# Weight units placed 128c+p, small products partly on GpSimd, and a new order for a fused attention and channel-mix kernel

## The chip, the core and the metric

The kernel runs on one core of a Trainium2 chip. The core has five engines with programs of their own: TensorE (PE in the profile), VectorE (DVE), ScalarE (ACT), GpSimd (POOL) and SyncE (SP), which here only issues transfers. The metric is the device time of one execution in microseconds (us), as the median of several runs.

## The reference

Two layers in float32. The first is attention with a polynomial feature map and no softmax, over 4 batches, 4 heads, 1088 positions and 32 columns a head; the second mixes channels, over 1088 positions of 128 columns.

```python
def phi(x):                                   # 32 columns -> 8 x 8 = 64 features
    a = einsum('rd,bhsd->bhsr', S1, x); b = einsum('rd,bhsd->bhsr', S2, x)
    return einsum('bhsi,bhsj->bhsij', a, b).reshape(..., 64)
kv = einsum('bhsf,bhsd->bhfd', phi(k), v);  z = phi(k).sum(axis=2)
x = einsum('bhsf,bhfd->bhsd', phi(q), kv) / (einsum('bhsf,bhf->bhs', phi(q), z) + 1e-6)
x = x, heads side by side                     # (4, 1088, 128)
xk = mu_k * x + (1 - mu_k) * x_prev;  xr = mu_r * x + (1 - mu_r) * x_prev    # x_prev: one position earlier
out = sigmoid(xr @ w_r) * (maximum(xk @ w_k, 0) ** 2 @ w_v)                  # 128 -> 1024 -> 128
```

## The kernel before

All work is cut into small tasks, each a function in the kernel. The text `ORDER` lists their calls; the kernel goes through it from left to right, and this sets the order of instructions on every engine, since each engine runs its own instructions in that order and waits on semaphores for what others make. An entry such as `f1.0.2@67` calls `f1(0, 2)` with PSUM banks 6 and 7; a last letter V, A or G in `relu.0.1.A` chooses DVE, ACT or POOL. A bank can be written again only when its last reader is done.

A batch b goes through these tasks.

- Keys. `turn.k` turns k in blocks on DVE (batches 0 and 2); `pt` and `ptev` do so on PE, with an eviction from PSUM, for batches 1 and 3. `kproj` multiplies by the two sketch matrices, `abev` evicts, `kp` forms the 64 features on DVE. `kvmm` sums features times v on PE; `kvev`, `kdmm` and `kvbm` evict, turn and evict the result. `zmm`, `zev`, `wmm` and `wsq` make from the same projections the matrix by which the denominator is computed.
- Queries. `turn.q` turns q on DVE, `abwt` and `abw` project it on PE, `abwev` evicts. `pw` multiplies two of the three projections elementwise, `den` sums and inverts, `an` multiplies by the inverse, `qp` forms the 64 features. They come in two parts (18 and 16 positions of 34 a row) for batch 0 and in one part (`0.34`) for the others. `qtt` and `qt` turn the features on PE, `qttev` and `qtev` evict.
- Attention's output. `xmm` multiplies by kv; `xev`, `xtev` and `xs` bring x into SBUF, with the shifted position. `xk` and `xkt` form the mixed input in bf16 on DVE, `xb` a bf16 copy for the gate.
- Channel mix. The positions of a batch make groups g = 2b and 2b + 1 of 512, and group 8 holds the 256 left over. For each group, `f1.g.c` (c = 0 to 3) makes two blocks of 128 hidden units from `xk` and the scaled weights `wk`; `relu` evicts them to bf16, `sq` squares two of them at once, `f2.g.c` multiplies by `wv`. `rr` and `sig` make the gate on PE and ACT; `fin` multiplies the two on DVE and issues the stores, four a group.

`wset` prepares the weights: `wset.1` scales w_k by 1 - mu_k and casts it to `wk`, `wset.2` does both halves of w_r, `wset.3` casts w_v to `wv`. [...] Which hidden unit lies at which place is free, as long as `wk` and `wv` agree. Before, block c held units 8p + c: `wk_f` is read with a step of NC = 8 columns, and partition p of `wv_f` gets eight rows of w_v that lie side by side in memory.

All loads are issued by SP, in the order k0, q0, v0, the first keys of the turned batches (`krow0`), k1, w_k, q1, v1, w_r, w_v, then k, q and v of batches 2 and 3. Stores of the first seven groups that finish go out on SP; those of the eighth alternate between SP and ACT; the store of group 8, the last, is on SP.

Of the kernel before, what the change touches and what calls it, by code (L numbers as in the profile page):

```python
# [24 lines left out]


ORDER = """
zz.8@7 turn.k.0.0 spe.1@0 turn.k.0.1 spe.0@1 sk wset.4 zz.3@3 kproj.0.0@2 kproj.0.1@1 abev.0.0.A turn.q.0.2 abev.0.1.A
zz.2@4 zmm.0@3 zev.0.V wset.0 zz.1@4 wmm.0 wsq.0 kp.0.1 zz.1@4 abwt.0@2 abw.0.0 kp.0.0 abw.0.1@3 abwev.0.0.A
pt.k.1.1@2 pw.0.0.18 pt.k.1.0@1 ptev.k.1.1.A den.0.0.18 kvmm.0.0@0 abwev.0.1.A ptev.k.1.0.A pw.0.18.34 kvmm.0.1  # L30
an.0.0.18 den.0.18.34 pt.k.1.2@1 kproj.1.0@2 qp.0.0 ptev.k.1.2.A wset.1.A kproj.1.1@1 an.0.18.34 kvev.0.A abev.1.0.A
qp.0.1 kdmm.0 qtt.0@3 abev.1.1.A qt.0.0@45 kvbm.0.A qttev.0.A wset.2.A kp.1.0 qt.0.1@67 qtev.0.0.A zmm.1@3 qtev.0.1.A
kp.1.1 xmm.0.0@45 kvmm.1.0@0 xtev.0.A xev.0.0.A xs.0.G zev.1.V xmm.0.1@67 xb.0.0.A xk.0.0 wmm.1 xev.0.1.A turn.q.1.2
f1.0.0@12 xb.0.2.G f1.0.1@45 xb.0.1.G relu.0.0.A kvmm.1.1 wsq.1 wset.3.G xk.0.1 abwt.1@3 relu.0.1.A abw.1.1@1
turn.k.2.2 f1.0.2@67 abwev.1.1.A abw.1.0 sq.0.0.A kvev.1.V pt.k.3.0@1 abwev.1.0.V pt.k.3.1@2 kdmm.1 ptev.k.3.0.V
f1.1.2@34 ptev.k.3.1.A kvbm.1.V rr.1@5 relu.0.2.A pw.1.0.34 pt.k.3.2@0 den.1.0.34 f1.1.3@12 ptev.k.3.2.A kproj.2.0@6
sig.1 an.1.0.34 kproj.3.1@0 relu.1.2.A qp.1.1 kproj.3.0@5 abev.2.0.A f2.0.0@7 abev.3.0.A qp.1.0 abev.3.1.A f2.0.1
relu.1.3.A f1.0.3@56 qt.1.1@34 turn.q.3.2 relu.0.3.A zmm.3@2 kproj.2.1@1 qtev.1.1.A sq.0.2.V qtt.1@0 f1.1.0@56 zev.3.A
abev.2.1.A qt.1.0@34 qttev.1.A xkt.0 kp.3.1 relu.1.0.A wmm.3 f1.1.1@01 qtev.1.0.A wsq.3 zmm.2@5 turn.q.2.2 abw.3.1@2
zev.2.A relu.1.1.A xmm.1.0@34 kp.3.0 abwt.3@6 xtev.1.A abw.3.0 xev.1.0.A xs.1.A abwev.3.1.A f2.0.2 xk.1.0 xb.1.0.G  # L40
abwev.3.0.A wmm.2 rr.0@2 sq.1.2.A pw.3.0.34 f1.2.0@34 wsq.2 den.3.0.34 f1.2.1@01 kvmm.3.0@5 an.3.0.34 sig.0 abwt.2@6
sq.1.0.V abw.2.0 relu.2.0.A abw.2.1@2 qp.3.0 abwev.2.0.A kvmm.3.1 abwev.2.1.A f2.0.3 kvev.3.A relu.2.1.A pw.2.0.34
kdmm.3 rr.2@6 fin.0 f1.2.2@23 kvbm.3.A kp.2.1 sig.2 qtt.3@4 xmm.1.1@01 relu.2.2.A qt.3.0@56 qp.3.1 xev.1.1.A f2.1.0@2
qttev.3.A qtev.3.0.A f2.1.1 xb.1.1.G xk.1.1 f1.2.3@34 sq.2.0.V f1.3.2@01 relu.2.3.A f2.1.2 qt.3.1@56 kp.2.0 relu.3.2.A
f2.1.3 qtev.3.1.A f1.3.3@34 fin.1 xmm.3.0@01 den.2.0.34 relu.3.3.A xmm.3.1@56 sq.2.2.V kvmm.2.0@2 xtev.3.A xev.3.0.A
kvmm.2.1 xs.3.A xev.3.1.A xk.3.0 xb.3.0.G f1.3.0@34 kvev.2.A rr.3@7 xk.3.1 xb.3.1.G relu.3.0.A kdmm.2 f1.3.1@01
an.2.0.34 f2.2.0@5 sig.3 sq.3.2.V f2.2.1 relu.3.1.A f1.6.0@34 qp.2.1 f2.2.2 relu.6.0.A f2.2.3 f1.6.1@01 fin.2 kvbm.2.A
qt.2.1@67 relu.6.1.A sq.3.0.V f1.7.1@23 qtev.2.1.A f1.7.0@01 qp.2.0 f2.3.0@5 relu.7.0.A f2.3.1 f2.3.2 sq.6.0.V qtt.2@4
relu.7.1.A f1.6.2@01 f2.3.3 qttev.2.V qt.2.0@67 xb.1.2.A sq.7.0.V relu.6.2.A f1.6.3@23 f2.6.0@4 qtev.2.0.V relu.6.3.A
f1.7.2@01 f2.6.1 xkt.1 relu.7.2.A sq.6.2.V xmm.2.0@67 xmm.2.1@23 xtev.2.A xev.2.0.A fin.3 xs.2.G f1.7.3@01 xev.2.1.A  # L50
xb.2.0.G f2.6.2 xk.2.0 relu.7.3.A f2.7.0@5 xb.2.1.G xk.2.1 f1.4.0@67 xb.2.2.A rr.6@0 relu.4.0.A sq.7.2.V f1.4.1@23
rr.7@1 sig.6 f1.4.2@67 relu.4.1.V sig.7 f2.7.1 relu.4.2.A f1.4.3@01 sq.4.0.V f2.6.3 f1.5.2@23 relu.4.3.A f1.5.0@67
fin.6 f2.7.2 relu.5.0.A f1.5.1@01 sq.4.2.V f2.7.3 relu.5.1.A f2.4.0@4 fin.7 f2.4.1 xkt.2 relu.5.2.A f2.4.2 xkt.3
sq.5.0.V f1.5.3@01 f1.8.0@56 relu.5.3.A f1.8.1@23 rr.4@7 relu.8.0.V f2.4.3 xb.3.2.A sq.5.2.V f1.8.2@01 relu.8.1.A
f2.5.0@5 sig.4 f2.5.1 f1.8.3@23 sq.8.0.V relu.8.2.A f2.5.2 fin.4 rr.8@7 relu.8.3.A rr.5@6 f2.5.3 sq.8.2.V sig.5
f2.8.0@4 f2.8.1 sig.8 fin.5 f2.8.2 f2.8.3 fin.8
# [8 lines left out]
def kernel(  # L65
# [147 lines left out]
    def scale(eng, o, i, f):  # L213
        if eng == "A":
            nc.scalar.activation(o, i, COPY, scale=f)  # L215
        else:
            nc.gpsimd.tensor_scalar(o, i, f, 0.0, op0=MUL, op1=ADD)

    def wset(i, eng="G"):
        if i == 4:  # L220
            nc.vector.tensor_mul(ZL[:], _ap(ps["s", 1][:, :D], [[0, 4], [1, D]]), _ap(mz[:], [[1, 4], [0, D]]))
            nc.vector.tensor_copy(mu[:], ps["s", 1][:, 64:66])
            nc.gpsimd.tensor_scalar(omu[:], mu[:], -1.0, 1.0, op0=MUL, op1=ADD)
# [1 line left out]
            nc.gpsimd.tensor_add(nzm[:], omu[:], tmp[:])
        elif i == 0:
            nc.vector.reciprocal(rat[:], nzm[:])
            nc.vector.tensor_mul(rat[:], rat[:], mu[:])
        elif i == 1:
            scale(eng, wk[:], _ap(wk_f[:], [[1, NC], [DFF // 2 + 4, 2], [NC, 64]]), nzm[:, :1])  # L230
        elif i == 2:
            scale(eng, wr[:, 0], wr_f[:], mu[:, 1:])
            scale(eng, wr[:, 1], wr_f[:], omu[:, 1:])
        else:
            copy(eng, wv[:].rearrange("p (y c) d -> p y (c d)", y=2), wv_f[:, :, :DFF // 2])

    def copy(eng, o, i):
        if eng == "A":
            nc.scalar.copy(o, i)  # L239
        else:  # L240
            (nc.gpsimd if eng == "G" else nc.vector).tensor_copy(o, i)  # L241
# [218 lines left out]
    def size(g):  # L460
        return 512 if g < 8 else 256

    def f1(g, cp, banks):
        i, j = banks
        n = size(g)
        h = ps["h", g, cp] = PS[:, i:j + 1:j - i, :n]
        if g < 8:
            x = sb["xk", g // 2, g % 2][:]
        else:
            x = XT[:].rearrange("p u b a -> p (u b a)")  # L470
        for c in range(2):
            nc.tensor.matmul(h[:, c, :], wk[:, 2 * cp + c].rearrange("p y f -> p (y f)"), x, skip_group_check=True)  # L472

    def relu(g, cp, eng):
        if cp % 2 == 0:
# [42 lines left out]
        nc.scalar.activation(r[:, :size(g)], ps["r", g][:, :size(g)], SIGMOID)  # L518

    fins = []  # L520

    def fin(g):
# [5 lines left out]
        nc.vector.tensor_mul(x[:, :n], ps["o", g][:, :n], x[:, :n])  # L528
        if g == 8:
            nc.sync.dma_start(out.rearrange("b (a u) f -> (b a) u f", u=U)[:, U - 2:, :], o[:, :2, :])  # L530
        for c in range(4 if g < 8 else 0):
            dst = out[g // 2].rearrange("(a u) f -> a u f", u=U)[:, 16 * (g % 2) + c:16 * (g % 2) + c + 13:4, :]
            queues[c].dma_start(dst, o[32 * c:32 * c + 32])
# [12 lines left out]

# [28 lines left out]
```

## Time and profile before

| | |
|---|---|
| median of 3 runs | 84.17 us (84.11 to 86.27) |
| profiled execution, its own time | 84.56 us |
| its span, from the first to the last instruction | 82.6 us |
| PE, DVE, ACT, POOL busy, share of the span | 92%, 87%, 78%, 11% |
| instructions | 3382 |
| bytes moved by DMA | 10.43 MB |
| granted clock of TensorE | 1.0 of full speed |

A line of a timeline or of the chain gives the start and the length in us, the engine, the tile and the line of the kernel; "x16" means that so many instructions are taken together. A line of the groups gives the busy time of all instructions of a kind and the mean time of one in ns. All lines are from one profiled execution. L239 and L241 are the lines of the helper `copy`, which many tasks share (ACT, and DVE or POOL); L215 is that of `scale`. f1 is L472, f2 L501, relu on ACT L480, sq L491 and L489, fin L528.

### The profile page before, as it was taken

How to read it: one execution, taken by the hardware profiler on the slowest of the kernel's cores; microseconds unless marked ns; L12 is line 12 of the kernel's file. 1: busy time of each engine (PE TensorE's matmuls, PEld its weight loads, DVE VectorE, ACT ScalarE, POOL GpSimd, SP SyncE). 2: the span in 40 equal slices, each digit the busy share in tenths (PEclk: the TensorE clock that was granted, in tenths of full speed). 3: DMA queues.
4: the chain of work that ended last, by engine and by line, in shares of the span. 5: the costliest groups of instructions: out<-in, count | busy, mean ns of one | idle time of the engine just before them, and what ended most of it. 6: DMA issues, size and time to landing. Idle time of an engine off the chain costs nothing.

```text
span 82.6 us, 3382 instructions
## 1 busy us (share of the span) xinstructions
...
## 2 busy tenths in 40 slices
...
GB/s 29 293 271 290 320 378 365 378 385 366 363 367 90 3 8 0 8 4 12 0 8 39 91 4 32 101 2 20 107 8 0 34 94 8 42 136 76 55 194 69
DMA packets 11441, 10.43 MB, mean 126 GB/s; under 512 B 1954, under 2 KB 9380, under 8 KB 11428
## 3 DMA queue, kind: packets, MB, share of 16 engines
...
q8 instruction: 11, 0.18, 0.9%
...
HBM read 8.00 MB, written 2.23 MB: 124 GB/s over the span
## 4 chain that ended last, share of the span: by engine, by line
PE 73%; ACT 8%; DMA 7%; DVE 4%; issue 1%; SPq 1%; DVEq 0%
PE ps L472 18%; PE ps L501 17%; PE ps L362 8%; DMA q<-in_q_dram 7%; PE ps L425 7%; PE ps L331 5%; PE ps L514 5%; PE ps L437 4%; PE ps L285 3%; ACT wk L215 3%; PE ps L267 3%; ACT qpT L239 2%; DVE qT L246 2%; SPq L124 1%; PE ps L349 1%
## 5 line engine op out<-in xcount | busy, mean ns | idle before, releaser
L480 ACT ACTIVATE k<-ps 128x1024 bf16<-128x1024 f32 (+1 forms) x34 | 32.8, 999 | 2.2 <-PE ps L472 1.7
L501 PEld LDWEIGHTS <-k 128*128 128x128 bf16 x272 | 16.6, 98 | 3.3 <-DVE k L491 0.2
L501 PE MATMUL ps<-wv,k 128*128 128x128 bf16 x272 | 18.6, 219 | 0.0
L491 DVE TENSOR_TENSOR k<-k 128x2048 bf16<-128x2048 bf16 (+1 forms) x16 | 18.3, 1149 | 0.3
L472 PE MATMUL ps<-xk,wk 128*128 128x512 bf16 x64 | 18.2, 379 | 0.1
L300 DVE TENSOR_TENSOR kp<-ab 128x1024 f32<-128x1024 f32 (+1 forms) x8 | 10.6, 1347 | 0.4 <-ACT ab L239 0.4
L398 DVE TENSOR_TENSOR qp<-an,abw 128x1152 f32<-128x1152 f32 (+1 forms) x8 | 10.1, 1279 | 0.1
L425 PE MATMUL ps<-ident,qp 128*128 128x128 f32 x64 | 8.3, 274 | 0.0
L239 ACT COPY qpT<-ps 128x1024 f32<-128x1024 f32 (+1 forms) x10 | 8.1, 831 | 0.0
L472 PEld LDWEIGHTS <-wk 128*128 128x128 bf16 x72 | 6.3, 101 | 2.3 <-issue 0.6
L425 PEld LDWEIGHTS ps<-ident,qp 128*128 128x128 f32 x64 | 7.0, 140 | 1.2 <-ACT q L518 0.4
L362 PE MATMUL ps<-SQ,qT 128*32 128x96 f32 (+1 forms) x160 | 7.4, 253 | 0.0
L241 POOL CAST XB<-X 128x512 bf16<-128x512 f32 (+1 forms) x7 | 4.4, 651 | 26.9 <-ACT X L239 26.9
L178 PE MATMUL ps<-zero 128*128 128x512 bf16 x15 | 5.8, 516 | 1.2 <-DVE warm L141 1.2
L362 PEld LDWEIGHTS ps<-SQ,qT 128*32 128x32 f32 (+1 forms) x160 | 6.5, 126 | 0.3
L445 DVE SCALAR_TENSOR_TENSOR xk<-ps,rat,X 128x512 bf16<-128x512 f32 x8 | 5.8, 743 | 1.0 <-ACT X L239 1.0
L246 DVE STREAM_TRANSPOSE qT<-q 128x1088 f32<-128x1088 f32 x4 | 5.2, 1304 | 1.2 <-DMA q<-in_q_dram 1.2
L239 ACT COPY abw<-ps 128x384 f32<-128x384 f32 (+1 forms) x7 | 3.3, 515 | 3.4 <-PE ps L362 3.4
L285 PEld LDWEIGHTS ps<-SK,kT 128*32 128x32 f32 (+1 forms) x234 | 5.3, 116 | 0.8 <-POOL SQ L211 0.4
L239 ACT COPY ab<-ps 128x320 f32<-128x320 f32 (+1 forms) x8 | 3.1, 444 | 3.5 <-PE ps L285 3.4
L285 PE MATMUL ps<-SK,kT 128*32 128x64 f32 (+1 forms) x234 | 5.8, 224 | 0.0
L528 DVE TENSOR_TENSOR q<-ps,q 128x512 f32<-128x512 f32 x8 | 5.5, 688 | 0.2
...
## 6 DMA issues: line engine op xcount, KB each, us to landing
...
kr<-in_k_dram SPq DMA_DIRECT2D x4, 256.0 KB, 7.5
...
```

What stands on the lines that cost most here:

```text
L178: nc.tensor.matmul(PS[:, banks[0], :], zero[:, :P], zero[:], skip_group_check=True)
L239: nc.scalar.copy(o, i)
L246: nc.vector.transpose(qT[b % 2][:].rearrange("p (w u) a -> p w (u a)", w=2), qin[b][:, :, :n])
L285: nc.tensor.matmul(_ap(o[c], *dst), kT[b % 2][:, m, c], SK[:] if b in TURNPE and m else SK[:].rearrange("p x h r -> p x (h r)"), skip_grou ...
L300: e.tensor_mul(o[:, :4 * (KG[j][1] - KG[j][0])], _ap(a_, list(a_.ap[1:]) + [[0, R]]), _ap(b_, [list(b_.ap[1]), [0, R], list(b_.ap[2])]))
L362: nc.tensor.matmul(_ap(o[c], [[6 * R, 4], [1, 3 * R]], c0), x[:, c], SQ[b][:].rearrange("p h r -> p (h r)"), skip_group_check=True, tile_p ...
L398: nc.vector.tensor_mul(o[:, :s1 - s0], _ap(a_, list(a_.ap[1:]) + [[0, R]]), _ap(b_, [list(b_.ap[1]), [0, R], list(b_.ap[2])]))
L425: nc.tensor.transpose(o[:, h // 2, c:c + P], sb["qp", b, hf][:, s:s + 2].rearrange("p s i j -> p (s i j)"), ident[:])
L472: nc.tensor.matmul(h[:, c, :], wk[:, 2 * cp + c].rearrange("p y f -> p (y f)"), x, skip_group_check=True)
L480: nc.scalar.activation(o, h, RELU)
L491: nc.vector.tensor_mul(o, k1, k1)
L501: nc.tensor.matmul(o[:, i * P:i * P + P], k2[:, 2 * (cp % 2) + c, i * P:i * P + P], wv[:, 2 * cp + c, :], start=(cp == 0 and c == 0 and i ...
```

## The change

Hidden unit 128c + p now lies in block c at place p. `wset.1` therefore reads neighbouring columns of `wk_f`, and `wv_f` is loaded with partition p taking row p of each block of 128 rows, in pieces of 512 bytes where it had pieces of 2 KB. Seven of the `pw` and `an` products go to GpSimd. In the stores of the eighth group to finish, the first stays on SP and the other three go to ACT, where they are issued after everything else in its program. `ORDER` is new as a whole; it lists the same tasks with one `zz` matmul fewer.

```diff
-    wv_f = const.tile([P, 2, DFF // 2 + 4], F32)
-    wk = const.tile([P, NC, 2, 64], BF16)
+    wv_f = const.tile([P, NC, P], F32)
+    wk = const.tile([P, NC, P], BF16)
...
-    nc.sync.dma_start(wv_f[:, :, :DFF // 2], moe_w_v.rearrange("(p y c) d -> p y (c d)", y=2, c=NC // 2))
+    nc.sync.dma_start(wv_f[:], moe_w_v.rearrange("(c p) d -> p c d", p=P))
...
-            scale(eng, wk[:], _ap(wk_f[:], [[1, NC], [DFF // 2 + 4, 2], [NC, 64]]), nzm[:, :1])
+            scale(eng, wk[:].rearrange("p (y c) f -> p y (c f)", y=2), wk_f[:, :, :DFF // 2], nzm[:, :1])
...
-            copy(eng, wv[:].rearrange("p (y c) d -> p y (c d)", y=2), wv_f[:, :, :DFF // 2])
+            copy(eng, wv[:], wv_f[:])
...
-            nc.tensor.matmul(h[:, c, :], wk[:, 2 * cp + c].rearrange("p y f -> p (y f)"), x, skip_group_check=True)
+            nc.tensor.matmul(h[:, c, :], wk[:, 2 * cp + c], x, skip_group_check=True)
...
-    fins = []
+    fins, late = [], []
...
-        queues = (nc.sync, nc.scalar) * 2 if len(fins) > 7 else (nc.sync,) * 4
+        queues = (nc.sync,) + (nc.scalar if len(fins) == 8 else nc.sync,) * 3
...
-            queues[c].dma_start(dst, o[32 * c:32 * c + 32])
+            if queues[c] is nc.scalar:
+                late.append((dst, o[32 * c:32 * c + 32]))
+            else:
+                queues[c].dma_start(dst, o[32 * c:32 * c + 32])
...
+    for dst, src in late:
+        nc.scalar.dma_start(dst, src)
```

The two orders from the first projections to where the third f1 pair stands (before, then after):

```
zz.2@4 zmm.0@3 zev.0.V wset.0 zz.1@4 wmm.0 wsq.0 kp.0.1 zz.1@4 abwt.0@2 abw.0.0 kp.0.0 abw.0.1@3 abwev.0.0.A
pt.k.1.1@2 pw.0.0.18 pt.k.1.0@1 ptev.k.1.1.A den.0.0.18 kvmm.0.0@0 abwev.0.1.A ptev.k.1.0.A pw.0.18.34 kvmm.0.1
an.0.0.18 den.0.18.34 pt.k.1.2@1 kproj.1.0@2 qp.0.0 ptev.k.1.2.A wset.1.A kproj.1.1@1 an.0.18.34 kvev.0.A abev.1.0.A
qp.0.1 kdmm.0 qtt.0@3 abev.1.1.A qt.0.0@45 kvbm.0.A qttev.0.A wset.2.A kp.1.0 qt.0.1@67 qtev.0.0.A zmm.1@3 qtev.0.1.A
kp.1.1 xmm.0.0@45 kvmm.1.0@0 xtev.0.A xev.0.0.A xs.0.G zev.1.V xmm.0.1@67 xb.0.0.A xk.0.0 wmm.1 xev.0.1.A turn.q.1.2
f1.0.0@12 xb.0.2.G f1.0.1@45 xb.0.1.G relu.0.0.A kvmm.1.1 wsq.1 wset.3.G xk.0.1 abwt.1@3 relu.0.1.A abw.1.1@1
turn.k.2.2 f1.0.2@67 ...

zz.2@3 zmm.0@0 zev.0.V zz.1@3 wmm.0 wset.0 wsq.0 zz.1@3 abwt.0@1 abw.0.0 abwev.0.0.A kp.0.1 abw.0.1@0 kp.0.0
pt.k.1.0@1 ptev.k.1.0.A pw.0.0.18.G pt.k.1.1@2 ptev.k.1.1.A kvmm.0.0@3 kvmm.0.1 wset.1.A kvev.0.A kproj.1.0@2 kdmm.0
kvbm.0.A abwev.0.1.V pw.0.18.34.G abev.1.0.A den.0.0.18 an.0.0.18.G den.0.18.34 pt.k.1.2@1 ptev.k.1.2.A qp.0.0
qt.0.0@45 qtev.0.0.A an.0.18.34.V qp.0.1 kp.1.0 kproj.1.1@3 abev.1.1.A kp.1.1 qtt.0@2 qttev.0.A wset.2.A qt.0.1@01
qtev.0.1.A xmm.0.0@23 xtev.0.V xev.0.0.A xs.0.G zmm.1@4 zev.1.A kvmm.1.0@5 kvmm.1.1 xk.0.0 turn.q.1.2 kvev.1.A
xb.0.0.A xmm.0.1@01 xev.0.1.A wmm.1 xb.0.1.G f1.0.0@23 f1.0.1@67 relu.0.0.A relu.0.1.A kdmm.1 wsq.1 abwt.1@4 abw.1.0
abwev.1.0.A abw.1.1@2 f1.0.2@67 rr.0@4 kvbm.1.A abwev.1.1.A pt.k.3.2@5 turn.k.2.2 relu.0.2.A wset.3.G pt.k.3.0@2
sq.0.0.V pt.k.3.1@3 ptev.k.3.2.A xk.0.1 pw.1.0.34.G ptev.k.3.0.A ptev.k.3.1.A f1.0.3@01 ...
```

Over the whole order these tasks change their engine:

| from, to | tasks |
|---|---|
| DVE to GpSimd | pw.0.0.18, pw.0.18.34, an.0.0.18, pw.1.0.34, pw.3.0.34, an.3.0.34, an.2.0.34 |
| ACT to DVE | abwev.0.1, xtev.0, xtev.1, xtev.2, xtev.3, sq.0.0, kvbm.2, xev.2.0, xev.2.1, relu.4.2 |
| DVE to ACT | zev.1, kvev.1, abwev.1.0, ptev.k.3.0, kvbm.1, qttev.2, qtev.2.0, relu.4.1 |
| ACT to GpSimd | xs.1, xs.3 |

The end of the two orders (before, then after):

```
f2.5.0@5 sig.4 f2.5.1 f1.8.3@23 sq.8.0.V relu.8.2.A f2.5.2 fin.4 rr.8@7 relu.8.3.A rr.5@6 f2.5.3 sq.8.2.V sig.5
f2.8.0@4 f2.8.1 sig.8 fin.5 f2.8.2 f2.8.3 fin.8

f2.4.3 relu.8.0.V f1.8.2@67 sq.5.2.V f2.5.0@3 rr.5@4 sig.4 fin.4 relu.8.1.A sq.8.0.V f1.8.3@01 f2.5.1 f2.5.2 f2.5.3
relu.8.2.A relu.8.3.A sq.8.2.V rr.8@0 sig.5 f2.8.0@1 fin.5 f2.8.1 sig.8 f2.8.2 f2.8.3 fin.8
```

49 lines of the change are left out of this document (20 added, 29 removed).

## The prediction

> **What bounds the kernel now.** I read the page first, then the stretches (busy microseconds of PE, PE's weight loads, DVE, ACT and POOL, clock, DMA share, GB/s), then the chain that ended last, in order of time.
>
> ```profile
> span 82.6 us, 3382 instructions
> 14.67:21.89 7.22, 6.32 (x124) 4.91 (x124) 5.74 (x8) 7.13 (x15) 0.21 (x1) 1.00 1.07 373
> 21.89:77.04 55.15, 55.15 (x1103) 42.89 (x1103) 54.32 (x72) 52.30 (x82) 5.85 (x10) 1.00 0.20 54
> 77.04:82.60 5.56, 1.32 (x24) 1.15 (x21) 1.64 (x3) 0.87 (x2) 0.00 (x0) 1.00 0.45 118
> ```
>
> From 21.89 us to 77.04 us PE is busy for the whole 55.15 us at full clock, DVE for 54.32 and ACT for 52.30. There PE's own work sets the pace and two engines stand close behind. So time can be had in three places: the entry before 21.89, the work that PE still has to do after it, and the tail after 77.04. POOL works 5.85 of 55.15 us.
>
> ```profile
> 14.67 2.16 ACT wk L215
> ...
> 16.98 0.60 ACT ab L239 x2
> ...
> 17.92 0.59 ACT wr L215 x2
> 18.51 1.81 ACT qpT L239 x2
> 20.32 0.68 ACT X L239 x2
> ...
> 21.09 0.76 DVE xk L445
> ...
> 21.89 1.02 PE ps L472 x4
> 22.91 0.58 PE ps L331 x32
> 23.50 0.12 PE ps L349 x16
> ...
> 77.06 0.61 ACT q L518
> 77.69 0.69 DVE q L528
> ...
> 78.46 0.42 DVE kr L528
> ```
>
> The chain runs through ACT from 14.67 to 21.00: the weight mix wset.1 (2.16 us), then every eviction that batch 0 needs, in ACT's program order, until xk.0.0 can form the first input of f1. At 21.89 the chain goes over to PE (f1.0.0) and stays there.
>
> **The change, part by part.** I follow each engine's program in the new order: an instruction starts when its engine is free and its inputs are there, and lasts as long as its row says.
>
> ```profile
> 9.47 2.62 DVE L300 TENSOR_TENSOR kp<-ab 128x1024 f32<-128x1024 f32 x2
> 11.13 0.52 ACT L239 COPY abw<-ps 128x432 f32<-128x432 f32 x1 [3.09 <-PE ps L362]
> 12.57 1.21 PE L331 MATMUL ps<-kp,v 128*32 128x64 f32 x72
> 14.10 2.12 PE L285 MATMUL ps<-SK,kT 128*128 128x64 f32 x18
> 17.31 1.91 PE L425 MATMUL ps<-ident,qp 128*128 128x128 f32 x16
> 21.76 1.30 DVE L246 STREAM_TRANSPOSE qT<-q 128x1088 f32<-128x1088 f32 x1
> 23.71 2.15 DVE L249 STREAM_TRANSPOSE kT<-k 128x576 f32<-128x576 f32 x2
> ```
>
> *Weight mix.* A row of the groups by shape (busy, mean ns of one, idle before):
>
> ```profile
> L239 ACT CAST XB<-X 128x544 bf16<-128x544 f32 x1 | 0.6, 645 | 0.1
> ```
>
> A mix of 1024 neighbouring columns on ACT is not in the trace. Below: 0.645 us, for 544 columns; above: the strided 2.16. I take 0.645 × 1024/544 = 1.2, from the nearest row. The mix also moves ahead of ptev.k.1.2, to about 13.1 us, where ACT had idle time: it ends at 14.3.
>
> *Entry, up to f1.0.0.* Until kp.0.0 ends (9.47 + 2.62 = 12.09) nothing of weight changes: one warm-up matmul less and spe.0 ahead of spe.1 lie before the arrival of q, for which DVE waits in both orders. PE then has pt.k.1.0, pt.k.1.1 and kvmm.0 (1.21, to 13.8), and now kproj.1.0 (10 of the 18 matmuls, 1.2) to 15.0 and kdmm.0. kvev.0 is done behind the mix at 14.5, so kdmm.0 does not wait. ACT takes kvbm.0 at 15.1, abev.1.0 (half of 0.60) and ptev.k.1.2. On PE qt.0.0 (half of 1.91) ends at 16.3, kproj.1.1 (8 of 18, 0.94) at 17.2, qt.0.1 at 18.2. ACT follows: qtev.0.0 to 17.2, abev.1.1 to 17.6, qttev.0 and wset.2 (0.59) to 18.4, qtev.0.1 (half of 1.81) to 19.3, xev.0.0 to 19.9. Then xk.0.0 (0.76) ends at 20.7. PE meanwhile does xmm.0.0, zmm.1, all of kvmm.1 (kvmm.1.1 was behind f1 before), xmm.0.1 and wmm.1, and comes free at about 21.0. **f1.0.0 starts at 21.0 in place of 21.89: −0.9 us**, and kvmm.1.1 is done by then, **−0.6** (0.58 in the chain).
>
> *Products on GpSimd.* Seven of the pw and an multiplications go to POOL. The trace has no two-input POOL product of that size.
>
> ```profile
> L225 POOL TENSOR_TENSOR nzm<-omu,tmp 128x2 f32<-128x2 f32 x1 | 0.2, 194 | 0.1
> L241 POOL CAST wv<-wv_f 128x1024 bf16<-128x1024 f32 x1 | 1.0, 1041 | 0.0
> L376 DVE TENSOR_TENSOR pw<-abw 128x272 f32<-128x272 f32 x3 | 1.3, 437 | 0.0
> L491 DVE TENSOR_TENSOR k<-k 128x2048 bf16<-128x2048 bf16 x14 | 17.0, 1215 | 0.3
> L241 DVE COPY kT<-ps 128x384 f32<-128x384 f32 x1 | 0.5, 547 | 0.0
> L398 DVE TENSOR_TENSOR qp<-an,abw 128x1152 f32<-128x1152 f32 x4 | 5.3, 1337 | 0.0
> ```
>
> POOL's rows give 0.194 us fixed and (1041 − 194)/1022 = 0.83 ns a column. So 272 columns cost from 0.42 us (one input's rate) to 0.65 (two inputs read in turn), 144 columns 0.31 to 0.43. I take the upper ends, since both inputs have to be read. [...] In the entry pw.0.0.18 runs from 11.7 beneath kp.0.0; abwev.0.1 is now on DVE (0.55, 12.1 to 12.6); pw.0.18.34 runs beneath den.0.0.18 and an.0.0.18 beneath den.0.18.34, so qp.0.0 starts at about 13.8 and, at 1.34 us, ends at 15.1. PE wants it at 15.4. They cost nothing there; with that cover gone, 0.1 to 0.3 each.
>
> *DVE and ACT after f1.0.0.* DVE loses four products (4 × 0.44 = 1.75). Onto it come sq.0.0 (1.22), two xev of 512 columns (about 0.7 each, from 0.547 for 384), three xtev and kvbm.2 (0.9 together, estimated from that row) and a relu; off it go qtev.2.0 (1024 columns, about 1.2), abwev.1.0 and ptev.k.3.0 (0.6 and 0.55), kvev.1, kvbm.1 and qttev.2 (0.3 each) and a relu of the same size: +0.3. DVE nets about −1.5 us. ACT gets the opposite of these and loses sq.0.0, which costs it more than DVE, and two xs: about −2. Both were within 1 to 3 us of PE, so this is cover for PE and no gain by itself: I count 0. xs.1 and xs.3 move to an idle POOL: 0.
>
> *A new wait at once behind f1.* DVE's order is xk.0.0, turn.q.1.2 (1.30), wsq.1; abwt.1 on PE needs wsq.1. In the old order kvmm.1.1 filled that time on PE. Now PE has f1.0.0, f1.0.1 (0.9) and kdmm.1 until 22.0, and abwt.1 comes at 22.3: **+0.3**. What is queued behind it on PE, abw.1.0 and abw.1.1, waits too. abwt.1 stood at 23.50 before, with kdmm.1 still to do, so the kernel is about 1.2 ahead there. Next, f1.0.3 needs the banks that xk.0.1 reads, and xk.0.1 now stands behind turn.k.2.2 (2.15) and sq.0.0: ready at 26.2 when PE comes at 26.1, so 0 to 0.3, of which I count nothing, because DVE's relief comes right behind it.
>
> *Weights 128c+p in the load of wv.* Its 256 pieces of 2 KB become 1024 of 512 B; the loads queued behind (k2, q2, v2, kr3, q3, v3) move with it.
>
> ```profile
> DMA packets 1467, 0.60 MB, mean 301 GB/s; under 512 B 1034, under 2 KB 1466, under 8 KB 1467
> ...
> DMA packets 423, 0.76 MB, mean 381 GB/s; under 512 B 25, under 2 KB 116, under 8 KB 423
> ...
> 15.55 1.43 SPq L130 DMA_DIRECT2D kr<-in_k_dram x2
> ...
> kr<-in_k_dram SPq DMA_DIRECT2D x2, 256.0 KB, 7.6
> ```
>
> These are windows 7 to 9 us and 11 to 13 us, with 16 full DMA engines (32 engine-us). One packet takes 21.8 ns at a mean of 409 B and 75.7 ns at 1797 B. On the line through both, 512 B cost 26 ns and 2 KB 85 ns: (1024 × 26 − 256 × 85)/16 = +0.3 us. The ends: −0.0 (21.8 ns) and +3.5 us (75.7 ns for a 512 B piece). kr3, issued by 16.3 us, landed about 23.9; its first reader pt.k.3.2 now stands at about 25.1 on PE. With +0.3 us it is covered: 0. [...]
>
> *Tail.* Only stores remain (DMA issues, and the last one's microseconds to landing).
>
> ```profile
> 76.89 2.74 SPq L533 DMA_DIRECT2D out_dram<-q  x6
> ...
> 79.73 0.40 SPq L530 DMA_DIRECT2D out_dram<-kr  x1
> ...
> out_dram<-kr SPq DMA_DIRECT2D x1, 128.0 KB, 1.8
> ```
>
> The last store waits behind SP's six (0.46 each): its data is ready at 78.88, its issue starts at 79.73. In the new order fin.5 leaves SP one store and ACT three, issued after ACT's last instruction, sig.8, so no compute stands behind them. fin.8's store can issue at once, at about 78.95; ACT's third store issues at much the same time. **−0.8 us.**
>
> *Sum.* −0.9 − 0.6 + 0.3 − 0.8 = −2.0 us. The profiled execution took 84.56 us, 1.96 more than its span, so it would become 82.6. It stood 0.39 above the median 84.17; against the median the forecast is 84.17 − 2.0 = **82.2 us**, 2.4% less. About 2% (1.7 us, the line at 82.5) is what a measurement of this kernel can tell from no change.
>
> **The rivals.**
>
> *A. More than forecast.* The relief of DVE (−1.5) and ACT (−2) also removes PE's small waits inside the 55.15 us. For: two engines there are over 94% busy. Against: the chain shows PE back to back. With half of DVE's relief gained, 82.2 − 0.8 = 81.4.
>
> *B. DVE's queue eats the lead.* wsq.1 and xk.0.1 come half a microsecond later each than I walked them. For: both stand behind long transposes (1.30, 2.15). Against: DVE was 98% busy and now has less to do. 82.2 + 1.0 = 83.2.
>
> *C. GpSimd holds up DVE.* DVE stands still while POOL multiplies: four products after f1, 4 × 0.65 = 2.6 us, more than the 1.75 they free. DVE, 98% busy, would then carry +1.1 us net and set the end: 82.2 + 1.1 = 83.3.
>
> ```profile
> 46.11 0.73 POOL L241 CAST XB<-X 128x512 bf16<-128x512 f32 x1 [7.32 <-ACT X L239]
> 46.29 0.74 DVE L445 SCALAR_TENSOR_TENSOR xk<-ps,rat,X 128x512 bf16<-128x512 f32 x1
> ```
>
> Against: xk takes 0.74 beside a working POOL and 0.76 at 21.09 beside an idle one. For: xk reads one operand from PSUM; DVE's two-input products beside POOL are not in the trace. [...]
>
> *D. The 512 B pieces cost what 2 KB pieces cost* (+3.5 us): kr3 lands at 27.4, and PE stands at pt.k.3.2 for 2.3 us: 84.5. It decides from +1.2 us on. Against: the 1034 small packets went through in 2 us.
>
> *E. Slower: PE stops for ACT in the relu pairs.* The new order issues many f1 pairs and their relus back to back (relu.6.2 and 6.3, 7.2 and 7.3, 1.2 and 1.1); the next f1 wants the banks of the first relu.
>
> ```profile
> L480 ACT ACTIVATE k<-ps 128x1024 bf16<-128x1024 f32 (+1 forms) x34 | 32.8, 999 | 2.2 <-PE ps L472 1.7
> ```
>
> A relu takes 1.0 us, two f1 matmuls about 0.45 and the f2 block between about as much. If PE stands for the remainder, 0.5 us, in each of eight groups, that is +4.0: 86.2. It ends slower than before once the eight waits exceed 0.25 us each. For: ACT is 95% busy, and no f1 can pass the one that waits. Against: ACT gets 2 us less to do.
>
> **How the numbers follow.** Forecast 82.2: 0.57, its own range 81.4 to 83.0, four fifths of it below 82.5. A 0.10, B 0.09, C 0.05, D 0.05, E 0.14. Faster by over 2%: 0.46 + 0.10 = 0.56. Slower by over 2%: 0.14, case E. Within 2%: 0.30. The range runs from 80.9 to 84.8: it holds A to D and leaves out most of E.
>
> **What would show it.** Right: wset.1 at 1.2 us, f1.0.0 near 21.0 us, a PE wait of some 0.3 us before abwt.1, the last store issued within 0.2 us of fin.8, DVE and ACT less full after 22 us. Wrong: qp or sq lengthened beside POOL (C), PE idle before pt.k.3.2 (D), PE idle before f1 on ACT again and again (E).

## The result, and the profile after

| | after | before |
|---|---|---|
| first comparison, median (4 runs each) | 85.49 us (85.23 to 86.85) | 85.22 us (84.11 to 86.32) |
| ratio, 95% interval | 1.0123 [1.0085, 1.0161] | |
| repeated on one chip (b1: 12 and 35 runs) | 85.34 us (84.0 to 87.11) | 85.56 us (83.9 to 86.72) |
| ratio, 95% interval | 0.9968 [0.9891, 1.0045] | |

The change makes no difference that could be measured; the 1.2% of the first comparison did not come back with more runs. The forecast was 82.2 us. The times of both kernels fall into groups by chance events that the experiments bring out (the point at which PE's matmuls get faster at the start and, in after, a late load of PE's instructions), so ratios use the runs within 1.5% of each kernel's fastest, and executions are compared below with the same outcome of these events.

The profiled execution of after took 85.23 us. First its busy instructions over the stretches that answer to before's (entry, body, tail):

```profile
span 83.4 us, 3382 instructions
14.61:22.69 8.08, 8.04 (x211) 6.64 (x200) 7.27 (x10) 6.58 (x17) 0.65 (x2) 1.00 1.10 356
22.69:79.40 56.71, 54.88 (x1082) 43.78 (x1092) 53.57 (x70) 52.49 (x81) 10.30 (x16) 1.00 0.20 51
79.40:83.40 4.00, 0.24 (x5) 0.06 (x2) 0.42 (x1) 0.00 (x0) 0.00 (x0) 1.00 0.46 128
```

The body was 55.15 us long with PE busy throughout; now it is 56.71 us with PE busy 54.88. PE's work is nearly the same, but it stands still for up to 1.8 us (ten matmul records are missing: x1082 beside x1092 weight loads). DVE and ACT are hardly less busy in it; POOL went from 5.85 to 10.30.

The timeline of ACT, then the body's longest waits of PE and its weight loads in the view of waits (total us, times, longest):

```profile
14.61 1.16 ACT L215 ACTIVATE wk<-wk_f,nzm 128x1024 bf16<-128x1024 f32 x1
```
```profile
PE ps L285 <- DVE SQ L322: 0.9, 1, 0.9
PE ps L472 <- DVE xk L445: 0.3, 1, 0.3
```
```profile
PEld ps L285 <- DVE SQ L322: 1.3, 1, 1.3
```

The weight mix takes 1.16 us in place of 2.16. One wait is new and large: kproj.2.1 (L285) waits for `SQ`, which wsq.3 on DVE writes.

The start of kproj.0 on PE, in the timelines of before, of after, and of a second execution of after (b1, 85.17 us):

```profile
6.38 1.21 PE L285 MATMUL ps<-SK,kT 128*32 128x64 f32 x72
```
```profile
6.85 2.15 PE L285 MATMUL ps<-SK,kT 128*32 128x64 f32 x72
```
```profile
6.20 1.21 PE L285 MATMUL ps<-SK,kT 128*32 128x64 f32 x72
```

The same 72 matmuls take 1.21 or 2.15 us. In before's and b1's profile the spacing of PE's matmuls drops to half at about 5.2 us, in after's only at about 9 us (`zz`, matmuls of zeros with 512 columns, start 0.42 us apart up to 4.15 us in before and after, then 0.22 apart at 5.6 us in before and b1, and still 0.40 at 5.9 us in after); abwt.0 then starts at 11.17 us in place of 9.70. The granted clock shows 1.0 in all three.

The tail of after (DVE, then the queues of ACT and SP):

```profile
79.42 1.36 ACTq L549 DMA_DIRECT2D out_dram<-q  x3
79.73 0.42 DVE L528 TENSOR_TENSOR kr<-ps,kr 128x256 f32<-128x256 f32 x1 [0.34 <-issue]
80.18 0.35 SPq L530 DMA_DIRECT2D out_dram<-kr  x1
```

fin.8's store is issued 0.03 us after fin.8 ends, as foretold. But ACT's three stores, a row of 1.36 us, are issued until 80.78. The profile has landings 2.2 us after an issue began for ACT's and 1.9 us for fin.8's, and the last data packets of the execution are on ACT's queue: its third store is now the last.

### The profile page after: what moved, and what is told of

Same layout as the page of the kernel before. It is cut to its first block, busy times and chain, and to the rows that moved or that the text cites. A ratio compares the mean times of both kernels' runs of the same rounds, so it can differ in the third digit from the quotient of the medians.

```text
span 83.4 us, 3382 instructions
## 1 busy us (share of the span) xinstructions
PE 76.1 (91%) x1471; PEld 58.8 (70%) x1482; DVE 70.3 (84%) x103; ACT 62.6 (75%) x102; POOL 15.0 (18%) x39
## 4 chain that ended last, share of the span: by engine, by line
PE 68%; ACT 20%; issue 4%; DVE 3%
PE ps L501 17%; PE ps L472 12%; ACT k L480 9%; PE ps L178 6%; PE ps L362 6%; PE ps L285 6%; ACT qpT L239 5%; PE ps L425 4%; PE ps L514 4%; PE ps L331 4%; PE ps L437 3%; ACT abw L239 2%; ACT X L239 1%; ACT q L518 1%; PE ps L267 1%
## 5 line engine op out<-in xcount | busy, mean ns | idle before, releaser
L491 DVE TENSOR_TENSOR k<-k 128x2048 bf16<-128x2048 bf16 (+1 forms) x17 | 19.4, 1151 | 0.0
L472 PE MATMUL ps<-xk,wk 128*128 128x512 bf16 x54 | 16.0, 379 | 0.6 <-DVE xk L445 0.3
L239 ACT COPY qpT<-ps 128x1024 f32<-128x1024 f32 (+1 forms) x12 | 9.4, 797 | 0.2 <-PE ps L425 0.2
L285 PEld LDWEIGHTS ps<-SK,kT 128*32 128x32 f32 (+1 forms) x234 | 6.2, 136 | 2.7 <-DVE SQ L322 1.3
L285 PE MATMUL ps<-SK,kT 128*32 128x64 f32 (+1 forms) x234 | 6.9, 253 | 0.9 <-DVE SQ L322 0.9
L239 ACT COPY ab<-ps 128x320 f32<-128x320 f32 (+1 forms) x8 | 3.1, 430 | 6.0 <-PE ps L285 6.0
L241 POOL COPY X<-X 128x31 f32<-128x31 f32 x4 | 0.8, 210 | 30.9 <-DVE X L241 30.9
L241 POOL CAST XB<-X 128x512 bf16<-128x512 f32 (+1 forms) x7 | 4.9, 696 | 7.9 <-DVE X L241 4.6
L239 ACT COPY abw<-ps 128x432 f32<-128x432 f32 (+1 forms) x7 | 3.5, 513 | 3.5 <-PE ps L362 3.4
```

Source lines behind the costliest of these rows:

```text
L285: nc.tensor.matmul(_ap(o[c], *dst), kT[b % 2][:, m, c], SK[:] if b in TURNPE and m else SK[:].rearrange("p x h r -> p x (h r)"), skip_grou ...
L472: nc.tensor.matmul(h[:, c, :], wk[:, 2 * cp + c], x, skip_group_check=True)
L491: nc.vector.tensor_mul(o, k1, k1)
```

## The experiments

### Is the start decided by the order of its tasks?

After begins with spe.0 ahead of spe.1 and has one `zz` fewer. Four kernels change only that (the second line of each pair is the new one):

```diff
a1 (after)   -spe.0@0 spe.1@1 turn.k.0.0 turn.k.0.1 sk zz.2@3
             +spe.1@1 spe.0@0 turn.k.0.0 turn.k.0.1 sk zz.3@3
a2 (before)  -spe.1@0 turn.k.0.1 spe.0@1 sk wset.4 zz.3@3
             +spe.0@1 turn.k.0.1 spe.1@0 sk wset.4 zz.2@3
a3 (after)   -zz.2@3
             +zz.3@3
a4 (after)   -spe.0@0 spe.1@1
             +spe.1@1 spe.0@0
```

> The changed kernel with the old start on TensorE: spe.1 ahead of spe.0 and three zero matmuls (zz.3) behind them. Theory P (the program's start decides when TensorE's matmuls go over to the short spacing): they do so near 5.2 us as in the kernel before, abwt.0 starts near 9.7 us in place of 11.17, and the time falls by about 1.5 us, to 83.7 to 84.0. Rival F (a window that runs freely against the program decides; the old profile drew an early one): the time stays at 85.2 to 85.6 in most runs, and early and late starts are drawn in both kernels.

> The kernel before with the new start on TensorE: spe.0 ahead of spe.1, and zz.2 in place of zz.3. Theory P: the short spacing comes only near 8.7 to 9.3 us, abwt.0 starts near 11.2 us, and the time is 1.5 us over the kernel before, about 85.6. Rival F: no steady difference, 84.1 in some runs and 86.3 in others, as the kernel before itself.

> The changed kernel with zz.3 in place of zz.2 alone. If the third zero matmul is what counts: 83.7 to 84.0. If the order of spe.1 and spe.0 counts: 85.3 to 85.6, since the third one comes at 6.7 us, behind the point at 5.2 us where the old profile turns fast. Rival F: as the changed kernel, whatever that draws.

> The changed kernel with spe.1 ahead of spe.0 alone (zz.2 kept). If the order of the two counts: about 83.8, as with the whole old start. If the third zero matmul counts: 85.2 to 85.6. Rival F: no steady difference from the changed kernel.

Measured: a1 85.8 us (ratio 1.0129 [1.0011, 1.0246]), a2 86.15 (1.0138 [1.0048, 1.0229]), a3 84.93 (0.9912 [0.9754, 1.0069]), a4 84.76 (0.9902 [0.9744, 1.0061]); before beside them 86.01. In the profiles a1, a2 and a4 have the late point (abw.0.0's weight loads begin at 11.77, 11.75 and 11.74 us; 11.42 in after), a3 the early one (9.84; 9.96 in before). So before's own start, put into after (a1), does not bring the early point, while before itself had it in its profile and spread from 84.31 to 86.63 there. a2's four times (85.83 to 86.27) alone would fit theory P, but a1's do not, and after and b1 are one program with a late and an early point. That the program's start decides fell; a point that is drawn anew in each execution stands. What draws it was not shown. By it f1.0.0 of after is 1.39 us later (22.69 against 21.30 in b1), 1.7% of the span.

b1 is after unchanged, with more runs. b2 and b3 put work that PE has to do anyway ahead of spe.1, to give PE less idle time there, in after and in before; b4 is b2 with three `xtev` on ACT.

```diff
b2 (after)   -zz.8@7 spe.0@0 spe.1@1 turn.k.0.0 turn.k.0.1 sk zz.2@3 kproj.0.0@2 wset.4
             +zz.5@7 spe.0@0 turn.k.0.0 sk turn.k.0.1 zz.3@7 spe.1@1 wset.4 kproj.0.0@2
b3 (before)  the same, with spe.0@1 and spe.1@0
b4 (as b2)   -xtev.0.V ... xtev.1.V ... xtev.3.V
             +xtev.0.A ... xtev.1.A ... xtev.3.A
```

> The changed kernel once more, unchanged, with more runs. Theory F (TensorE's short spacing begins at a free-running point, early near 5.3 us or late near 9.5 us, whatever the program): its runs fall into two heaps, about 84.0 with an early point and about 85.3 with a late one, beside single runs 1.0 to 1.5 us longer in which TensorE waits for its own instructions. The kernel before has heaps at 84.1 and 86.1. Rival P2 (the changed kernel always starts late): no run below 85.0.

> The changed kernel with the small matmuls of the start taken apart: spe.0 after five zero matmuls, sk between the two halves of turn.k, three more zero matmuls, then spe.1 and kproj at once. kproj then starts near 5.9 us and is done by 8.0 us even at the long spacing, before q's transpose ends at 8.4. Theory F: abwt.0 starts at 9.5 to 9.7 us in every run, the upper heap is gone, and the time is 83.7 to 84.2. Rival P2 or a rival in which long spacing goes on into abw.0: 85 and more in some runs.

> The kernel before with the same start as the run above. Theory F: it stays near 84.0 to 84.2 in all runs without the heap at 86.1, so that its difference to the run above is the change without its start: I expect it 0 to 0.3 us slower than the changed kernel with that start. If the change itself is worth the 2.0 us that was forecast, the difference is 2 us.

> The changed kernel with the new start, and xtev.0, xtev.1 and xtev.3 back on ACT. Theory: xtev.1 on DVE waits for xev.1.0 on ACT (1.1 us in the profile), wsq.3 stands behind it on DVE, and kproj.2.1 on TensorE behind that; with xtev on ACT the wait before kproj.2.1 (1.35 us) falls to 0.4 or less, and the time falls by 0.3 to 0.9 us against the kernel with the new start. Rival: TensorE catches up on a later wait anyway (DVE or ACT is the bound there): the wait before kproj.2.1 shrinks, the time stays within 0.2 us.

Measured: b1 as in the table above, with two times below 85.0 (84.0 and 84.23), so rival P2 fell; b2 86.83 us (1.0061 [0.9983, 1.0139]), b3 85.88 (0.9994 [0.9945, 1.0044]), b4 85.42 (1.0069 [1.0014, 1.0124]). All three profiles with the new start have the late point (abw.0.0's weight loads begin at 11.80, 11.62 and 11.62 us), and their times still spread over 1.8 to 3.9 us: a miss, the start could not be fixed this way. b4's profile showed kproj.2.1 0.9 us earlier than b2's, which led to c1.

### The wait before kproj.2.1

ACT, DVE and PE's weight loads of after around xtev.1 (L241), xev.1.0 (L239), wsq.3 (L322) and kproj.2.1 (L285):

```profile
36.76 0.58 ACT L239 COPY X<-ps 128x512 f32<-128x512 f32 x1
37.37 0.23 DVE L241 COPY X<-ps 128x64 f32<-128x64 f32 x1 [1.12 <-ACT X L239]
37.51 0.18 DVE L322 TENSOR_TENSOR SQ<-ps,m 128x32 f32<-128x32 f32 x1
...
37.75 0.49 PEld L285 LDWEIGHTS ps<-SK,kT 128*32 128x32 f32 x32 [1.35 <-DVE SQ L322]
```

In the new order xtev.1 is on DVE behind ACT's xev.1.0, both writing the same tile. DVE stands still for 1.12 us, wsq.3 stands behind it in DVE's program, and PE waits 1.35 us for the bank that wsq.3 reads. c1 puts this one task back on ACT, ahead of xev.1.0, and alternates the stores of fin.5.

```diff
-xev.1.0.A xtev.1.V xs.1.G
+xtev.1.A xev.1.0.A xs.1.G
-queues = (nc.sync,) + (nc.scalar if len(fins) == 8 else nc.sync,) * 3
+queues = (nc.sync, nc.scalar if len(fins) == 8 else nc.sync) * 2
```

> After, with xtev.1 on ScalarE ahead of xev.1.0, and fin.5's four stores issued alternately by SP and ScalarE in place of one and three. Theory X (the lost 0.9 us of the middle is one wait: DVE's xtev.1 waits for ScalarE's xev.1.0, wsq.3 stands behind it, kproj.2.1 waits for wsq.3): PE's idle time before kproj.2.1 goes from 1.35 us to about 0.45, and everything that PE does behind it comes 0.9 us earlier. Rival Y (ScalarE is the bound there anyway): the idle time moves to another place of PE before abw.3.1 and the gain is under 0.3 us. Tail: the last of ScalarE's stores ends its issue about 0.45 us earlier, and the span behind PE's last matmul is 0.3 to 0.5 us shorter than in after; if it is not, the landing time of SP's stores sets the end.

c1's timeline:

```profile
36.15 0.18 DVE L322 TENSOR_TENSOR SQ<-ps,m 128x32 f32<-128x32 f32 x1
36.74 0.70 ACT L239 COPY X<-ps 128x64 f32<-128x64 f32 x2
36.79 0.49 PEld L285 LDWEIGHTS ps<-SK,kT 128*32 128x32 f32 x32 [0.41 <-DVE SQ L322]
```

The wait is 0.41 us, and kproj.2.1 and all PE tasks up to abw.2.1 start 0.96 us earlier than in after. Theory X stands. The time was 84.5 us (83.45 to 85.96; before 86.14; 0.995 [0.9886, 1.0013]). The tail's part missed: the span ends 4.43 us after f2.8.3's weight loads begin, 4.21 in after, because SP is still at its second store of fin.5 (until 80.71) when fin.8's is ready (80.59).

### The stop inside abw.2.0

In b1's profile, and in those of a1, a3, a4, b2, b4 and c1 too, PE stops within abw.2.0 with nothing to wait for ("issue"). PE and its weight loads in b1, then the stretch from the start to 46.9 us with the number of weight loads in the third column (x986):

```profile
45.99 0.34 PE L362 MATMUL ps<-SQ,qT 128*32 128x96 f32 x6
47.32 0.63 PEld L362 LDWEIGHTS ps<-SQ,qT 128*32 128x32 f32 x26 [1.20 <-issue]
47.33 0.85 PE L362 MATMUL ps<-SQ,qT 128*32 128x96 f32 x26 [0.99 <-issue]
```
```profile
0.00:46.90 46.90, 43.15 (x980) 32.84 (x986) 39.74 (x62) 34.20 (x61) 11.46 (x32) 1.00 0.59 182
```

abw.2.0 takes 1.7 to 2.2 us in these profiles and 0.66 in after's. PE's instructions come in packets of 16 KB on a DMA queue of their own (q8 in after's profile: 11 packets, 0.18 MB). In b1 one starts at 44.68 and ends at 46.11, and PE goes on at 47.33; in after's profile the same packet starts at 43.70, 2.4 us earlier if the later start of that execution is taken off. The stores of fin.0 and fin.1 are issued just there, so c2 issues them behind fin.2's. c3 leaves them and adds 48 tiny matmuls (`fill`, 32 x 32 in the trace, not the 32 x 64 of the expectation) in PE's idle time before kproj.2.1.

```diff
c2  -queues[c].dma_start(dst, ...)
    +(held.append((dst, ...)) if g < 2 else queues[c].dma_start(dst, ...))   # held: issued after fin.2's
c3  -xmm.1.1@56 xb.1.0.G kproj.2.1@4
    +xmm.1.1@56 xb.1.0.G fill.48@2 kproj.2.1@4
```

> After, with the eight stores of fin.0 and fin.1 put behind those of fin.2 in SP's program, so that none is issued between 40 and 50 us. PE's stop inside abw.2.0 (0.9 to 1.5 us, in most executions) comes with a late 16 KB load of PE's instructions. Theory S (the stores hold up that load): the load starts at matmul pair 850 or so in place of 900, and abw.2.0 takes 0.66 us. Theory D (PE runs through 150 small matmuls in 2.5 us there and is at the end of what is loaded before the next load can be through): the load still starts at pair 900 and abw.2.0 still takes 1.7 to 2.2 us.

> After, with 48 tiny matmuls (32 x 64) put on PE in its idle time before kproj.2.1, so that each later border between instruction loads comes 48 pairs earlier in the work. They take about 0.7 of the 1.33 us of idle time and cost PE nothing. Theory D: the load is started before kvmm.3.0 and not in it, PE has 0.5 us of another wait in between, and the stop shrinks from 0.9 to 1.5 us to under 0.4. Theory S: the stop stays 0.9 us or more, at kvmm.3.1, 48 pairs earlier.

c2: what DMA moves from 40 to 50 us is one instruction packet, and the stop is still there, at the same weight load:

```profile
DMA packets 1, 0.02 MB, mean 2 GB/s; under 512 B 0, under 2 KB 0, under 8 KB 0
...
q8 instruction: 1, 0.02, 0.8%
```
```profile
47.75 0.35 PE L362 MATMUL ps<-SQ,qT 128*32 128x96 f32 x6
49.06 0.85 PE L362 MATMUL ps<-SQ,qT 128*32 128x96 f32 x26 [0.97 <-issue]
```

Theory S fell. In c3 the line for abw.2.0 is whole, and a small stop (0.34 us of the weight loads) stands elsewhere, at pair 859 (a pair is a weight load and its matmul), 127 before 986:

```profile
47.81 0.85 PE L367 MATMUL ps<-SQ,qT 128*32 128x96 f32 x32
```
```profile
41.43 0.76 PEld L506 LDWEIGHTS <-k 128*128 128x128 bf16 x13 [0.34 <-issue]
```
```profile
0.00:41.30 41.30, 39.51 (x858) 29.38 (x859) 33.39 (x54) 27.17 (x52) 9.79 (x30) 1.00 0.62 196
```

Times: c2 85.72 us (1.0069 [0.993, 1.0207]), c3 84.73 (1.0019 [0.9951, 1.0086]).

So there are borders every 127 or 128 pairs (859 to 986, 220 to 348), fixed in number and not in task, at which PE can run dry. The work between two borders can be read from a trace: the stretch up to 986 holds 4.72 us in before and 2.35 in after, whose order puts kvmm.3 and abw.2, 152 pairs of small matmuls, in a row. e1 and e2 move the borders by 20 pairs in after and by 52 in before, again in idle time of PE (tiny matmuls of 32 x 32).

```diff
e1 (after)   -xmm.0.0@23 xtev.0.V
             +xmm.0.0@23 fill.20@6 xtev.0.V
e2 (before)  -qp.0.1 kdmm.0
             +qp.0.1 fill.52@3 kdmm.0
```

> After, with 20 tiny matmuls (32 x 32, 0.2 us together) on PE in its idle time before zmm.1, so that every later border of an instruction load (pairs 732, 859, 986, 1113 in the traces) comes 20 pairs earlier in the work. Theory D (a chunk of 127 pairs can't be passed in under some 3.1 us, because the load of the next one is asked for at a border): by after's trace the chunk up to pair 986 then holds 4.2 us of work in place of 2.35, and no other chunk behind the entry under 3.7: no stop, abw.2.0 takes 0.66 us in the profile, and the upper times of after (86.8 to 87.1) are gone; lowest times as in after, 84.0. Rival: the stop in abw.2.0 comes with the task and not with the border, and stays at 0.9 to 1.5 us.

> Before, with 52 tiny matmuls (32 x 32, 0.57 us together) in PE's 0.96 us of idle time before kdmm.0. By before's trace the chunk between the borders at pairs 859 and 986 then holds 2.1 us of work in place of 4.7. Theory D: PE stops for 0.8 to 1.5 us at pair 986, which is in kvmm.3.1, in the profile and in most timed runs, and the times rise by about that (lowest 84.0 to about 85). Rival: the stop belongs to after's order (its tasks or its engines); before shows none and its times stay.

e2's PE, the weight loads at its other stop, and its counts up to the two (x987, x476):

```profile
42.99 0.51 PE L336 MATMUL ps<-kp,v 128*32 128x64 f32 x23
43.90 0.33 PE L336 MATMUL ps<-kp,v 128*32 128x64 f32 x9 [0.39 <-issue]
```
```profile
26.07 0.75 PEld L367 LDWEIGHTS ps<-SQ,qT 128*128 128x128 f32 x6 [0.98 <-issue]
```
```profile
0.00:43.60 43.60, 40.81 (x986) 30.17 (x987) 36.20 (x64) 32.01 (x55) 5.50 (x24) 1.00 0.57 186
0.00:25.60 25.60, 23.37 (x475) 16.38 (x476) 19.67 (x39) 14.81 (x27) 4.86 (x23) 1.00 0.96 312
```

Before has the stop now, in kvmm.3.1 as foretold: that task takes 1.15 us in place of 0.55. The size was less than foretold (0.6 for 0.8 to 1.5), and a second stop of 1.0 us came at another border, in abw.1.0, which was not foretold. e2 took 86.48 us (1.0259 [1.0176, 1.0342], lowest 85.97 for before's 83.95). In e1 abw.2.0 is whole again (0.66 us), but two borders in the entry cost 0.5 to 0.6 us each in that profile, and its times (85.47, 84.37 to 87.14; 1.0057 [0.9998, 1.0116]) kept their upper end: half a miss. In all 19 profiles, the stops of PE over 0.5 us behind 10 us that are not put down to another engine or to a transfer lie at pairs 220, 348, 476, 986 and 987.

The work between two borders is not the whole rule: e2's stop at pair 476 came behind 5.9 us of work. The same traces show what is. Taken in order, the first ten 16 KB packets of each profile belong to the borders from pair 220 to 1367, 190 in all. At the 22 that PE reached less than 1.4 us after the packet had landed, its weight loads stopped for 0.15 to 1.55 us and went on 1.2 to 1.6 us after the landing. At the 168 that it reached later there is no stop over 0.3 us that is not put down to another engine. Behind 26 us a packet starts between 1.4 us before and 1.7 us after PE passes the border before; ahead of that, while the inputs are still loaded, 1.8 to 4.3 us after it. What sets these starts was not tested, nor why after's profile has 1.4 us before at pair 859 and b1's 1.0 us after.

The packets are of 16 KB, and the 127 pairs between two borders are 254 instructions. The border inside abw.2.0 costs PE's weight loads 0.9 to 1.6 us in 8 of the 9 profiles of after's order with unshifted borders.

### Taking both losses away, and two parts by themselves

e3 is after with `fill.20` as in e1 and c1's two edits. e4 is e3 with all seven products of `pw` and `an` on DVE (`.G` to `.V`). f1 is e3 with the stores of fin.5 as in after. c4 is before with the weight units alone: the diff's lines on wv_f, wk and f1, with order, engines and stores as they were.

> After, with both losses taken away: 20 tiny matmuls before zmm.1 (no stop in abw.2.0), xtev.1 on ScalarE ahead of xev.1.0 (wait before kproj.2.1 0.4 in place of 1.35 us), and fin.5's stores alternately from SP and ScalarE. If the two causes and the random point of matmul spacing are all that kept the forecast from coming true, it runs 0.9 us below after's undisturbed times and never has the stop: 83.2 at its lowest (early spacing) and 84.5 (late), against 84.1 and 86.3 of before. If a third cause is there, it stays at 84.0 or above at its lowest.

> As e3, with all seven products of pw and an on VectorE in place of GpSimd. The prediction counted the move to GpSimd as cover for PE and 0 by itself, apart from 0.1 to 0.3 us for each of three in the entry. Expected by that: 0 to 0.4 us slower than e3, by a later qp.0.0. Rival: the products on GpSimd (0.7 to 1.5 us each beside VectorE) delay qp, and back on VectorE it is 0.2 to 0.8 us faster.

> As e3, with the stores of fin.5 as in after (one on SP, three late on ScalarE). If the alternate stores cost something, as c1's profile says (SP still issues a store of fin.5 when fin.8's data is ready), the last store is issued within 0.1 us of fin.8's end, in place of 0.2 later, and times are 0.2 to 0.3 us below e3's: 83.1 at the lowest. If ScalarE's three stores set the end, they are 0.2 to 0.4 above e3's.

> Before, with the weight units placed 128c+p alone (new load of wv, weight mix over neighbouring columns); order, engines and stores as before. The prediction's first term: wset.1 takes 1.16 us in place of 2.16, and f1.0.0 starts 0.5 to 0.9 us earlier against abwt.0 (12.2 us between the two before), because the chain up to f1.0.0 ran through wset.1. Rival: PE's program before f1 (qt, zmm, xmm) or DVE's sets it and it moves under 0.3 us. In both the 512 B pieces of wv cost nothing that PE sees.

| | median, range (us) | before beside it | ratio, 95% interval |
|---|---|---|---|
| e3 | 84.96, 83.36 to 86.7 | 86.01 | 0.9903 [0.9839, 0.9967] |
| f1 | 84.22, 83.36 to 84.99 | 86.08 | 0.9839 [0.9751, 0.9926] |
| e4 | 86.32, 84.8 to 87.54 | 86.01 | none |
| c4 | 85.03, 84.81 to 85.54 | 86.14 | 1.01 [1.0055, 1.0144] |

With both losses gone the new order beats before: f1 in two groups, 83.36 to 83.71 and 84.73 to 84.99, against 84.31 to 84.77 and 86.08 to 86.67 of before (one run of before, 85.38, lies between). Between the means of the groups that is 1.1 and 1.7 us. f1's last store is issued 0.04 us after fin.8 and its tail is 4.23 us, as in after (4.21); e3's is 4.37. The alternate stores cost 0.1 to 0.2 us, less than the 0.2 to 0.3 expected of f1, and the lowest times are equal.

e4, the longest waits of PE in the body and entry:

```profile
PE ps L477 <- DVE xk L450: 0.7, 1, 0.7
PE ps L430 <- DVE qp L403: 0.3, 1, 0.3
```

With the products on DVE, qt.0.0 waits for qp.0.0 and f1.6.0 for xk.3.0: 0.9 us together. The median is 1.4 above e3's, and so is the lowest time; for the rest of that no cause was found. The rival (GpSimd delays) fell; the expected 0 to 0.4 was too small, since it had only the entry.

c4, ACT's mix and a wait of PE:

```profile
15.92 1.15 ACT L215 ACTIVATE wk<-wk_f,nzm 128x1024 bf16<-128x1024 f32 x1
```
```profile
PE ps L267 <- DMA kr<-in_k_dram: 1.2, 1, 1.2
```

From pt.k.1.1 to f1.0.0 (starts of the weight loads) c4 takes 8.82 us, before 9.83: the shorter mix is worth 1.0 us, as forecast, since the stretch from its end to f1.0.0 is nearly the same (5.11 and 5.06 us). Against abwt.0, as the expectation had it, f1.0.0 came later (12.6 us for 12.2), because pt.k.1.1 began 1.30 us late: k1 landed 7.5 us after its issue; in 17 other profiles it was 5.4 to 6.1, in e3's 6.9. In c4's profile the gain is eaten, and f1.0.0 is 0.3 us later than in before. All six times of c4 lie between before's two groups, so its median is below before's and its ratio, which goes by the lower group, above 1: what the weights alone are worth in time is not shown. Whether the 512 B pieces, queued behind k1, slow it now and then was not settled.

## Why the prediction was wrong

It is judged on b1 against before's profile; both have the early point. The entry of b1 (DVE, PE), then the start of abwt.1 in before:

```profile
19.91 0.75 DVE L445 SCALAR_TENSOR_TENSOR xk<-ps,rat,X 128x512 bf16<-128x512 f32 x1 [0.73 <-ACT zs L239]
21.80 0.15 DVE L322 TENSOR_TENSOR SQ<-ps,m 128x32 f32<-128x32 f32 x1
...
21.30 1.03 PE L472 MATMUL ps<-xk,wk 128*128 128x512 bf16 x3
22.16 0.27 PE L340 MATMUL ps<-ident,kvs 128*128 128x128 f32 x1
22.36 0.32 PE L349 MATMUL ps<-SQ,qT 128*32 128x24 f32 x16
```
```profile
23.32 0.30 PE L349 MATMUL ps<-SQ,qT 128*32 128x24 f32 x16
```

- **Entry.** The mix took 1.15 us (forecast 1.2) and xk.0.0 ended at 20.66 (forecast 20.7). f1.0.0 started at 21.30 in place of 21.0, 0.6 earlier than before and not 0.9. PE was the late one: kvmm.1 lost 0.45 us at the border at pair 348.
- **kvmm.1.1 ahead of f1, and the new wait.** The first was right, the wait did not come: wsq.1 ended at 21.95 (forecast: abwt.1 held until 22.3), before kdmm.1 (L340) began, and PE ran on without a stop. abwt.1 started at 22.36, near the forecast's 22.3, by luck: f1.0.0 was 0.3 us late and the wait of 0.3 us was missing. That is 0.96 earlier than before; the forecast's 1.2 took 23.50 from the chain, where abwt.1 had begun at 23.32.
- **"three xtev ... I count 0".** This step failed. The sum took the moved evictions by their busy time and called DVE's and ACT's program cover. DVE's relief did come (71.9 us busy before, 70.3 after), but not where PE needed it. xtev.1 on DVE must wait for ACT, and DVE's order carries that wait to wsq.3 and to PE: 0.96 us by c1. It is the lead of the entry, lost.
- **A term that was missing.** The order of PE's tasks was costed by the tasks' durations alone. That 152 small matmuls in a row outrun the loads of instructions was in no step and no rival: 1.3 us in b1. Without it f2.8.3 would load its weights at 77.8; in before it does at 77.92.
- **Tail.** From that point to the end of the span 4.67 us became 4.21 in after: −0.5, not −0.8. The step saw that fin.8's store is free and put ACT's third store "at much the same time"; in after's profile that one ends its issue at 80.78, 0.25 after fin.8's, and lands last.
- **The sum.** −0.1 at PE's end without the stop, −0.5 in the tail: −0.6, not −2.0; with the stop +0.7 or +0.8, which is b1's span (83.4 against 82.6). f1's profile has neither loss, but stops of 0.32 and 0.65 us at pairs 220 and 348, and its f1.0.0 starts at 21.92, so the entry's lead is gone; with 0.4 from the tail its time is 83.71 us for before's 84.56.
- **The random point.** before's profile and two of its three times were of the early kind, so the base 84.17 was a lucky one: with 35 runs its median is 85.56.

**The rivals.** A did not come, and B not where it was put (wsq.1, xk.0.1); the wait at wsq.3 is of its kind. C fell, as e4 shows; the groups of POOL's products in after (busy, mean ns), then the longest one and the `kp` beside it:

```profile
L390 POOL TENSOR_TENSOR an<-abw,den 128x272 f32<-128x272 f32 x2 | 2.2, 1084 | 1.5 <-DVE den L383 1.5
L376 POOL TENSOR_TENSOR pw<-abw 128x272 f32<-128x272 f32 x2 | 1.5, 772 | 1.7 <-ACT abw L239 1.7
L398 DVE TENSOR_TENSOR qp<-an,abw 128x1152 f32<-128x1152 f32 x4 | 5.5, 1375 | 0.0
```
```profile
42.63 1.16 DVE L300 TENSOR_TENSOR kp<-ab 128x1024 f32<-128x1024 f32 x1
42.79 1.51 POOL L390 TENSOR_TENSOR an<-abw,den 128x272 f32<-128x272 f32 x1 [1.55 <-DVE den L383]
```

They cost more than the upper end taken (0.65): one of them 1.51 us, 0.51 of it behind the end of a `kp` that DVE had begun before it, while the other took 0.66. DVE's `kp` of that shape took 1194 ns on average (1217 in before), and its `qp` grew only from 1337 to 1375 ns. The one held up is POOL, not DVE. D did not come at kr3: PE does not wait before pt.k.3.2. E did not come: none of PE's longer waits is for ACT's relus.
